# Eight order strings rewritten in a fused RWKV6 attention and GELU-MLP kernel

## The chip, the core and the metric

The kernel runs on one core of a Trainium2 chip. The time is the device time of one execution in microseconds (us). The median of three runs of the kernel before is given with its smallest and largest value. One further execution was recorded by the hardware profiler, and all views of the profile come from it.

A core has a matrix engine (TensorE, PE in the profile; its weight loads are shown as an engine of their own, PEld), a vector engine (VectorE, DVE), a scalar engine (ScalarE, ACT), GpSimd (POOL) and SyncE (SP), which in this kernel issues nearly all transfers. Each engine carries out its own list of instructions in order and waits at semaphores for the others. On TensorE the list is made of weight loads and matmuls; one fp32 matmul of the program shows as two weight loads and two matmuls in the trace, which is why the counts of the trace are twice those of the source.

## What is computed

There are four sequences of 768 tokens with eight heads of 48 channels. Each head runs a recurrence over time, and its output is the input of an MLP with the exact GELU:

```python
for t in range(S):                       # attention, per batch and head
    cur = einsum('bhd,bhe->bhde', u * kt, vt)
    y[:, :, t] = einsum('bhd,bhde->bhe', rt, state + cur)
    state = wt[..., None] * state + einsum('bhd,bhe->bhde', kt, vt)
x = y.transpose(0, 2, 1, 3).reshape(3072, 384)
h = x @ w_in                             # (384, 2048)
g = 0.5 * h * (1 + erf(h / sqrt(2)))
return g @ w_out                         # (2048, 384)
```

The weights come to the device in double precision and are turned to fp32 on the chip.

## The kernel before, in words

**Blocks.** The 3,072 tokens are cut into eight blocks of 384, and the program has one loop for each: in loop x the attention of block x runs beside the MLP of block x - 1. Within a block time is cut into chunks of 64 tokens, and the heads go in pairs, 12 chunk pairs for two pairs of heads.

**Attention of a block.** First the kernel lets VectorE multiply decay factors over growing stretches of time (`tot_sb`). In loops 0 and 1 the products of k and r within a chunk are then built level by level: TensorE multiplies blocks (`products`, L452, into a PSUM tile `d`), VectorE or ScalarE copies the valid part into `a_sb` (L513, L516), VectorE scales r and k with the decay (an `update`, L494 and L505), and the next level follows. Loops 2 to 7 use a shorter form with bursts of quarter blocks (L579, L588, copied at L604 and L621), ahead of which VectorE forms u r k (L391) and similar sums. Then come the transposes of k (L685, copied by ScalarE at L687 into `kx`), the products of k and v (L711, tile `kv_ps`), the chain of states on VectorE (L726, tile `st`), the part of y inside the chunks (L752, tile `y_ps`), two small copies that work as a fence on `y_ps` (L762, L764), the part of y from the states (L797), and the copies of y into `xT`, which the MLP reads. Some rows of y get to their place by small transfers on SP's and ScalarE's queues (L827). Loop 0 splits its attention into two units of two head pairs each, so that work can start when half of the data is there, and issues short matmuls on zeros (`keep_warm`, L225) between them.

**MLP of a block.** Block 0 goes through plain products: 16 steps of six matmuls in the trace into `h_ps` (L1059) with a GELU on ScalarE after each, then steps for the output (`o_ps`, L1153). Later blocks take a form with fewer multiplications, made of sums of weights (`w_sums` and `h_sums`, L844 to L888) and sums of x (`sums_of_x`, L897): products into `h_ps` and `u_ps` at L929, into `o_ps` at L1073.

**Weights.** w_in and w_out are 16 pieces of 768 KB. A piece is loaded by SP into a `raw` buffer (five of them; L200, the first three in shares of 256 KB at L205, each share behind a small memset on VectorE at L204). A conversion is three activations on ScalarE (L333, L334, L336) and two operations on VectorE (L345, L349), and its end issues the load of a later piece. So the order of the conversions also sets when SP issues loads. The rkw data of the next block are loaded in nine transfers of 384 or 256 KB (L176, `load`); those of block 1 in eight shares of 288 KB, each behind a memset on VectorE (L163 and L164, `load_second`).

**Where the order comes from.** All of this is written as generators that stop (`yield`) between steps; running a generator to its next stop issues the instructions of one step on all their engines. The string `PLAN[x]` decides, character by character, which generator takes its next step in loop x:

```python
for c in PLAN[x]:
    next(streams[c], None)
```

At the end of the string what is left in the loop's streams is run in a fixed order. The characters are:

- `.` a step of the MLP of block x - 1 (in loop 0: a step of unit 0 of the attention of block 0)
- `s` a step of the attention of block x (in loop 0: unit 1)
- `f` one of the first steps of the attention of block x + 1
- `l` a load for the next block (in loop 0: the gated shares of raw and of rkw)
- `c` a step of the conversions of weights (loops 0 and 1)
- `w` a step of the sums of weights (in loop 0: the load of v for block 1)
- `x` a step of the sums of x (in loop 0: matmuls on zeros)
- `p` in loop 0, the ScalarE part of a conversion alone

A step's instructions go to the ends of their engines' lists. The same steps in another order therefore do the same work, but each engine meets its waits in another order, and the transfers are issued at other places.

Of the kernel before, what the change touches and what calls it, by code (L numbers as in the profile page):

```python
# [36 lines left out]
NC_SP = 8  # L37
HALFWAY = 2
PLAN = {
    0: ".s...sl.ll.lclsllllssssl.lsl.l.ssl.lls..ssssc..s.sclcs.s..s..s.s.ss.s..csps.s.s.fpcfw",  # L40
    1: (
        "cs.c.cc.sslclcc.cs..ccswcc.sswccc.cccs.c.cccss.ccc.sc.scwlcclcsc.css.cs.clscsscclccc.sclls"
        "lc.wcc.ccfcccf.cc.s...fc.wcc.swcc.cc...cf.w.wwwx.xwxf.wl.f.xx"
    ),
    2: (
        "sw..sl..wss.....s..sws....ssw.wsw.sw.w.ss.lss..s.sw.ll.sw.s...ssls.s.s.ls..ss.s....s...sss"
        ".lsll.f.s.fs.ff..x.xl.xfxx"
    ),
    3: (
        "l.s.s..s...sls.ss....s...s.sss.ss.ss.ss...s.ssss..sssssssll....s....l..sl.sssls..llsf..sf."  # L50
        "ff.x.l.x.xfxx"
    ),
    4: (
        "sss...s..l....sl.s..s.s...l.ss..sss.l.s.s.ss.s.s...s.sl.ssl...sssss..s.....s.s..lss.sllfsf"
        "..lfs.f.f.x.x.xfxx"
    ),
    5: (
        ".ss...sss.l.....ss....sl.sssslss.s......sslss.sss..sssss..s..sl..s..s...s.lslsll.ssf.ff.s."
        ".x..x.lxxx"
    ),  # L60
    6: (
        "lls...ssss.s.s.s......l.s.s....s..sss.ssss.ss..sll..s...s..s..sss.s.sl.ss..s....slss.sl.lf"
        ".sf.f.s.ff..xx.xfxlx"
    ),
    7: "ss.ss.....s..s..s....s.ssss.ss...ss.s.ss..sss..sssss..s..s...s..s..s.s.sss..s.x..x..xxx",
}


# [1249 lines left out]
```

## Time and profile before

| | before |
|---|---|
| three runs | 590.59, 592.62 and 592.70 us; median 592.62 us |
| profiled execution | 592.35 us |
| its span, first to last instruction | 590.5 us |
| mean granted TensorE clock | 0.994 |
| TensorE busy, matmuls | 573.7 us (97%) |
| TensorE busy, weight loads | 521.3 us (88%), beside the matmuls |
| VectorE busy | 424.3 us (72%) |
| ScalarE busy | 290.8 us (49%) |
| GpSimd busy | 58.7 us (10%) |
| moved by DMA | 55.09 MB in 62,430 packets |

How to read it. "Busy" is the time within the span in which an engine carried out a counted instruction. The list of waits gives for an engine and a source line what the engine waited for ahead of that line: us in total, number of waits, the longest. "Issue" stands where the profile shows nothing that the engine waited for. Rows of the timeline give the start, the time, the engine, line, operation, output and input tiles and the number of instructions drawn together, with the idle time before them and its releaser in brackets. Rows of the windows give a stretch of time and its length; then busy time and number of instructions of TensorE's matmuls, its weight loads, VectorE, ScalarE and GpSimd; then the granted clock, the busy share of the DMA engines and the GB/s. Rows of the DMA queues give packets, MB and the share of the DMA engines' time in the window. Rows of the transfers give the issuing queue, the count, the KB of one and the median us from issue to landing. Rows of the groups give, behind the count, the busy time, the mean ns of one, and the idle time before them.

### The profile page before, as it was taken

The page shows a single profiled execution, that of the slowest core. Times are in us where ns is not written, and L with a number is a line of the kernel's source. Part 1 is how long each engine was busy: PE and PEld are TensorE (multiplying, and loading weights), DVE is VectorE, ACT ScalarE, POOL GpSimd, SP SyncE. Part 2 cuts the span into 40 slices and gives each one's busy share as a digit, 9 for nine tenths or more (in the row PEclk, how much of TensorE's full clock was granted, in tenths as well). Part 3 has the DMA queues.
Part 4 walks back from the last instruction along what each step waited for, and adds up shares of the span by engine and source line. Part 5 has one row for each costly group of instructions (what it writes and reads, how often), then busy time and mean ns, then how long its engine had stood idle before and what let it go on. Part 6 is the DMA issues. An engine that isn't in the chain of part 4 may idle for free. (4 is left out here: it accounts for less than half of the span.)

```text
span 590.5 us, 17675 instructions
## 1 busy us (share of the span) xinstructions
PE 573.7 (97%) x7616; PEld 521.3 (88%) x7616; DVE 424.3 (72%) x825; ACT 290.8 (49%) x668; POOL 58.7 (10%) x63
## 2 busy tenths in 40 slices
PE   6789999999999999999999999999999999999997
PEld 3476666699999989999999999999999999999997
DVE  6778768998959985687859986588859987420332
ACT  2258798535452467145652367246560466435400
POOL 3100000012000130011100130003100111003100
PEclk8999999999999999999999999999999999999999
DMA  7729645153232542445223432445213332114201
GB/s 253 255 80 319 214 159 163 44 125 80 26 68 68 122 56 37 132 145 100 29 54 116 107 53 42 111 138 92 28 34 108 81 48 40 30 44 54 28 13 35
DMA packets 62430, 55.09 MB, mean 93 GB/s; under 512 B 32400, under 2 KB 47504, under 8 KB 62352
## 3 DMA queue, kind: packets, MB, share of 16 engines
q1 hardware_dynamic: 50832, 45.62, 25.6%
q0 software_dynamic: 11424, 8.26, 10.7%
q8 instruction: 60, 0.98, 0.7%
q14 instruction: 18, 0.15, 0.1%
q10 hardware_dynamic: 96, 0.07, 0.1%
HBM read 36.24 MB, written 4.72 MB: 69 GB/s over the span
## 5 line engine op out<-in xcount | busy, mean ns | idle before, releaser
L929 PE MATMUL h_ps<-xT,w_in_sb 128*128 128x192 f32 x560 | 111.7, 331 | 0.7 <-DVE o_sb L1196 0.7
L980 POOL DMA_DIRECT2D g<-o_sb x42 | 50.7, 1250 | 482.0 <-ACT o_sb L965 473.4
L929 PEld LDWEIGHTS h_ps<-xT,w_in_sb 128*128 128x128 f32 x560 | 92.9, 190 | 5.0 <-ACT g L961 1.6
L929 PE MATMUL u_ps<-s,w_in_sb 128*128 128x192 f32 x224 | 41.2, 327 | 0.0
L1073 PE MATMUL o_ps<-w_out_sb,g 128*128 128x192 f32 x224 | 39.8, 326 | 0.0
L929 PEld LDWEIGHTS u_ps<-s,w_in_sb 128*128 128x128 f32 x224 | 37.1, 190 | 0.2
L1073 PEld LDWEIGHTS o_ps<-w_out_sb,g 128*128 128x128 f32 x224 | 37.0, 190 | 0.0
L604 ACT COPY a_sb<-d 32x256 f32<-32x256 f32 (+8 forms) x90 | 32.6, 363 | 4.2 <-PE d L588 2.7
L452 PEld LDWEIGHTS d<-rkw 64*64 64x64 f32 x1152 | 20.0, 142 | 16.1 <-issue 13.1
L1059 PE MATMUL h_ps<-xT,w_in_sb 128*128 128x384 f32 x96 | 32.6, 492 | 0.0
L1073 PE MATMUL o_ps<-w_out_sb,f 128*128 128x192 f32 x176 | 31.9, 330 | 0.0
L726 DVE SCALAR_TENSOR_TENSOR st<-st,tot_sb,kv_ps 128x48 f32<-128x48 f32 x160 | 29.0, 257 | 3.8 <-PE kv_ps L711 3.7
L1073 PE MATMUL o_ps<-t,g 128*128 128x192 f32 x176 | 31.3, 330 | 0.0
L1073 PE MATMUL o_ps<-t,s 128*128 128x192 f32 x176 | 31.3, 328 | 0.0
L1073 PE MATMUL o_ps<-w_out_sb,e 128*128 128x192 f32 x176 | 31.2, 328 | 0.0
L1073 PE MATMUL o_ps<-t,e 128*128 128x192 f32 x176 | 30.7, 327 | 0.0
L621 DVE COPY_PREDICATED a_sb<-quarter,d 128x480 f32<-128x480 uint8 (+5 forms) x54 | 23.1, 439 | 10.4 <-PE d L588 9.2
L1073 PEld LDWEIGHTS o_ps<-t,g 128*128 128x128 f32 x176 | 28.6, 190 | 0.5
L1073 PEld LDWEIGHTS o_ps<-w_out_sb,f 128*128 128x128 f32 x176 | 28.7, 190 | 0.4
L1073 PEld LDWEIGHTS o_ps<-t,s 128*128 128x128 f32 x176 | 28.8, 190 | 0.3
L1073 PEld LDWEIGHTS o_ps<-w_out_sb,e 128*128 128x128 f32 x176 | 28.8, 190 | 0.2
L1073 PEld LDWEIGHTS o_ps<-t,e 128*128 128x128 f32 x176 | 28.9, 190 | 0.1
(163 smaller groups left out, 1153.7 us busy)
## 6 DMA issues: line engine op xcount, KB each, us to landing
rkw<-in_rkw_dram SPq DMA_DIRECT2D x54, 256.0 KB, 3.6
g<-o_sb POOLq DMA_DIRECT2D x42, 192.0 KB, 3.6
raw<-in_w_out_dram SPq DMA_DIRECT2D x8, 768.0 KB, 4.7
v_in<-in_v_dram SPq DMA_DIRECT2D x8, 584.0 KB, 4.1
raw<-in_w_in_dram SPq DMA_DIRECT2D x5, 768.0 KB, 8.6
out_dram<-o_sb SPq DMA_DIRECT2D x20, 192.0 KB, 2.0
rkw<-kx SPq DMA_DIRECT2D x72, 48.0 KB, 2.0
rkw<-in_rkw_dram SPq DMA_DIRECT2D x6, 384.0 KB, 5.8
```

The source lines that it names most:

```text
L452: nc.tensor.matmul(d[half[p], g, n * width:(n + 1) * width], lhsT=kc[half[g], b, i, p], rhs=right(half[g], b, i, p), start=True, stop=True)
L604: nc.scalar.copy(out=at[z, g, first:behind, (a + 1) * h:], in_=d[z, :, :, to] if g == slice(None) else d[z, :, to])
L621: nc.vector.copy_predicated(out=an[:, :, :, :, (a + 1) * h:], mask=mask.to_broadcast(data.shape), data=data)
L726: nc.vector.scalar_tensor_tensor(out=stq[:, q, c], in0=stq[:, q, c - 1] if c else b4[:, q, NC - 1], scalar=totq[:, q, c:c + 1], in1=kvs[q ...
L929: nc.tensor.matmul(o, lhsT=lhsT, rhs=rhs, start=start, stop=True, skip_group_check=True)
L980: nc.gpsimd.dma_start(out=g, in_=z, accum_op=ALU.add)
L1059: nc.tensor.matmul(h_ps, lhsT=w_in_sb[:, f // FI, j, f % FI * 128:(f % FI + 1) * 128], rhs=xT[:, j, :], start=(j == 0), stop=(j == NJ - 1))
L1073: nc.tensor.matmul(o, lhsT=lhs(j), rhs=rhs(j), start=start and j == 0, stop=(j == HF - 1), skip_group_check=True)
```

## The change

Only the eight strings of `PLAN` are replaced. All steps stay what they are, and each stream holds the same steps in the same order among themselves; what differs is how the streams are interleaved. The whole diff:

```diff
--- before.py
+++ after.py
@@ -37,32 +37,32 @@
 NC_SP = 8
 HALFWAY = 2
 PLAN = {
-    0: ".s...sl.ll.lclsllllssssl.lsl.l.ssl.lls..ssssc..s.sclcs.s..s..s.s.ss.s..csps.s.s.fpcfw",
+    0: "l.s....llsl.lssslslss.lc.l.slslls...ssss..lcs.s.s.l.ss..ss..sccs.c.s.llpssslw..cs.ffpcc",
     1: (
-        "cs.c.cc.sslclcc.cs..ccswcc.sswccc.cccs.c.cccss.ccc.sc.scwlcclcsc.css.cs.clscsscclccc.sclls"
-        "lc.wcc.ccfcccf.cc.s...fc.wcc.swcc.cc...cf.w.wwwx.xwxf.wl.f.xx"
+        "..ccswccc.csl.scscs.s.sccwsc.clccs.ccsccc.csc.lscclswwclc.scs.wcssw.ss.cclcsc.ccs.lclccsc."
+        "ccclfccccccfccfcccccfccfccwf.ff......fw.sl.w.x.wx...x..x...xww"
     ),
     2: (
-        "sw..sl..wss.....s..sws....ssw.wsw.sw.w.ss.lss..s.sw.ll.sw.s...ssls.s.s.ls..ss.s....s...sss"
-        ".lsll.f.s.fs.ff..x.xl.xfxx"
+        "s.s.....ss....ssw.ws.wl.wsss.wws.s..lsl...lws.w..s.ww....s.s..l..sss.lssss....s..s..s.sls."
+        "llsf.sf.fs..fl.xx.x.fxx"
     ),
     3: (
-        "l.s.s..s...sls.ss....s...s.sss.ss.ss.ss...s.ssss..sssssssll....s....l..sl.sssls..llsf..sf."
-        "ff.x.l.x.xfxx"
+        "ls.ls....lss..ss.....ss..l.s.lsss.sss.s.s.s.ss..sss..sssssss....s.s..l...s..l.sslslsf.ffs."
+        "..x.lx..xxx"
     ),
     4: (
-        "sss...s..l....sl.s..s.s...l.ss..sss.l.s.s.ss.s.s...s.sl.ssl...sssss..s.....s.s..lss.sllfsf"
-        "..lfs.f.f.x.x.xfxx"
+        "lls.s.sss..s.l.........ssss.....sss.s.ss.s..s.sllss...s.s..l.sss.ss..s.ss...s..sslsll.s..f"
+        ".sf.sf..ff..xx.xflxx"
     ),
     5: (
-        ".ss...sss.l.....ss....sl.sssslss.s......sslss.sss..sssss..s..sl..s..s...s.lslsll.ssf.ff.s."
-        ".x..x.lxxx"
+        "..ss...s..ssl....sls...s.sss..sss..sss.sls...sllss..sssss.s..l..s.s...s.slll..s.ssfsf.fsf."
+        "....xxx.lxx"
     ),
     6: (
-        "lls...ssss.s.s.s......l.s.s....s..sss.ssss.ss..sll..s...s..s..sss.s.sl.ss..s....slss.sl.lf"
-        ".sf.f.s.ff..xx.xfxlx"
+        "ss..sss...s.....s.sl..s...l.s.ssls.s.s..s..sssssl......ss.ssss.sl.sl...s.....ss..llsssl.f."
+        "s.fsf.f.f.xx.l.xffxx"
     ),
-    7: "ss.ss.....s..s..s....s.ssss.ss...ss.s.ss..sss..sssss..s..s...s..s..s.s.sss..s.x..x..xxx",
+    7: "....ss.s...s.s.s....s.sss..ss.ss.sss..s..sss..sssssss......s.s....s..ssss.s...x.x..xxx",
 }
 
 
```

Read against the lists of the engines, it comes to this. In loop 0 TensorE's list is the same. The first share of raw (`l`) comes ahead of the first products, and the other shares are spread singly between steps of the attention; the VectorE halves of a conversion (L345, L349) come before the last two updates (L494), and the second pair of copies at L513 comes between the two copies at L687. In loop 1 the first five steps of the MLP of block 0 (L1059), which stood together behind the second products, are spread between the levels of the attention, with two ahead of the second products; conversions of weights shift by some steps, and three of the `f` steps stand behind the transposes of k. In loop 2 the first burst of quarters (L588) comes some steps earlier and the sums at L844 later. In loops 3 to 7 steps of `o_ps` (L1073) move across the products of k and v, the y products and the state products, four matmuls of the program at a time; in loop 5 the fence comes behind the four operations at L391 of the next block.

## The prediction

> **What bounds the kernel now.** I read the page's busy times first, then the waits of TensorE, then the order in time of loop 0, and last the DMA queues in short windows.
>
> ```profile
> PE 573.7 (97%) x7616; PEld 521.3 (88%) x7616; DVE 424.3 (72%) x825; ACT 290.8 (49%) x668; POOL 58.7 (10%) x63
> PE d L452 <- issue: 3.2, 2, 2.3
> PE kv_ps L711 <- issue: 1.5, 1, 1.5
> PE y_ps L752 <- DVE st L726: 1.3, 4, 0.4
> PE kv_ps L711 <- ACT kx L687: 0.6, 2, 0.3
> ```
>
> TensorE is busy 573.7 us of the span of 590.5. The changed program holds the same TensorE work, so only idle time can come or go: 16.8 us, of which the rows above carry the largest parts that order can touch. The two "issue" rows are unusual: TensorE has work, waits for no engine, and stands still. What they are shows in counts of instructions and in the queue that carries instructions:
>
> ```profile
> q8 instruction: 60, 0.98, 0.7%
> 0.00:18.80 18.80, 13.13 (x349) 7.88 (x350) 13.86 (x53) 6.67 (x9) 7.99 (x21) 0.91 0.79 254
> 0.00:25.00 25.00, 17.29 (x476) 10.43 (x477) 19.29 (x63) 6.67 (x9) 7.99 (x21) 0.93 0.85 283
> 0.00:43.10 43.10, 32.33 (x986) 21.99 (x989) 31.51 (x101) 15.82 (x27) 7.99 (x21) 0.92 0.60 199
> 0.00:46.60 46.60, 35.83 (x1113) 24.47 (x1114) 34.61 (x107) 18.04 (x32) 7.99 (x21) 0.93 0.60 195
> ```
>
> In each row the two counts behind the first times are TensorE's matmuls and weight loads. The first two windows end inside the two L452 gaps: 699 and 953 have begun, a step of 254. Queue q8 brings 60 packets for 15,232 of them, 254 each. So TensorE stops at a packet's edge when the next packet has not come. By steps of 254 to 255 further edges fall at about 1717, 1972 (loop 1 starts at 43.1, with 1975) and 2227 (46.6). When the packet comes late:
>
> ```profile
> q1 hardware_dynamic: 763, 1.46, 103.8%
> q8 instruction: 1, 0.02, 29.4%
> 25.85 0.62 PE L452 MATMUL d<-rkw 64*64 64x64 f32 x26 [2.27 <-issue]
> q1 hardware_dynamic: 763, 1.57, 85.0%
> q8 instruction: 1, 0.02, 18.5%
> ```
>
> The first q1 row is the window 19.4 to 23.4: no q8 packet, 1.46 MB of loads. Its q8 row is the window 23.4 to 23.6. TensorE had crossed the edge before at 19.4 and ran on at 25.85. The second pair is 46.75 to 52.3 and 52.3 to 52.6: the edge at 2227 is crossed at 46.75, and again 1.57 MB of loads go first. I read from both: a packet is asked for when the edge before it is crossed, goes behind the loads that are already issued, and can be used 2.4 us after it starts (23.45 to 25.85).
>
> **The change part by part.** No operation is added or removed; orders alone differ.
>
> Loop 0, loads. Before 21.6 us the old order issues eight shares of raw (256 KB) and eight of rkw (288 KB). The new one puts the first raw share ahead of the block products and spreads the others singly; by the same step on VectorE six and six are out. That is two of each less, 1.11 MB (from the KB below). Of the 1.46 MB ahead of the packet 0.35 are left, so the wait of 4.1 us falls to about 1.0 and the packet is usable at 19.4 + 1.0 + 2.4 = 22.8, before its need at 23.6 (25.85 less 2.27). The gap of 2.27 us goes. The gap at 18.8 is hidden today behind VectorE; I book nothing for it.
>
> ```profile
> rkw<-in_rkw_dram SPq DMA_DIRECT2D x8, 288.0 KB, 5.6
> raw<-in_w_in_dram SPq DMA_DIRECT2D x9, 256.0 KB, 5.6
> 22.47 0.60 PE L225 MATMUL warm<-zeros 128*128 128x512 bf16 x2
> 26.40 0.89 PE L225 MATMUL warm<-zeros 128*128 128x512 bf16 x2
> 23.88 0.55 DVE L516 COPY_PREDICATED a_sb<-mask,d 128x384 f32<-128x384 uint8 x1
> 26.50 0.96 DVE L505 TENSOR_TENSOR rkw<-rkw,tot_sb 128x768 f32<-128x768 f32 x1 [2.08 <-PE d L452]
> 31.20 0.93 PE L452 MATMUL d<-rkw 64*64 64x64 f32 x48
> 33.59 0.95 ACT L513 COPY a_sb<-d 32x384 f32<-32x384 f32 x2 [0.45 <-PE d L452]
> 33.90 1.47 PE L685 MATMUL kt_ps<-ident,rkw 128*128 128x128 f32 x12
> 34.76 1.50 ACT L687 COPY kx<-kt_ps 128x768 f32<-128x768 f32 x2 [0.21 <-PE kt_ps L685]
> 35.61 0.92 PE L711 MATMUL kv_ps<-v_in,kx 64*64 64x48 f32 x48 [0.23 <-ACT kx L687]
> ```
>
> What is late next is VectorE. After L516 ends at 24.43 come L505 (0.96), L516 (0.55) and two L505 (1.92): 27.9. The last block products follow, 28.5 to 29.4 (0.93 after a warm pair of 0.60), the update of k (half an L505, 0.5), kt at 30.0, its copy by ScalarE 0.86 later (34.76 less 33.90), 0.75 long. The new order has two L513 copies (0.95) between the two L687 copies, and kv waits for them: 30.9 + 0.75 + 0.95 + 0.2 = 32.8 in place of 35.61, a lead of 2.8. L345 and L349 move ahead of the last two updates; VectorE then ends near 33, before kv is done, so they cost nothing. The gap of 1.5 at the next edge has no load beside it (kv crosses its edge and the packet comes in its own time): it stays. Bounds of the lead: 0 if the packet is still late, 3.7 if nothing but TensorE counts (2.27, and 1.4 of matmuls that ran slowly after the gap, as 0.89 against 0.60 shows).
>
> Loop 1, start. Two mlp steps (four of the five were grouped) now come before the second 96 products.
>
> ```profile
> 46.07 0.44 PEld L452 LDWEIGHTS d<-kx,rkw 64*64 64x64 f32 x24 [0.42 <-ACT kx L401]
> 55.96 1.60 PE L452 MATMUL d<-rkw 64*64 64x32 f32 x96
> 44.68 1.47 PE L225 MATMUL warm<-zeros 128*128 128x512 bf16 x6
> 48.02 8.01 PE L1059 MATMUL h_ps<-xT,w_in_sb 128*128 128x384 f32 x24
> xT<-ysb ACTq DMA_DIRECT2D x3, 24.0 KB, 4.2
> 42.02 1.87 SPq L827 DMA_DIRECT2D xT<-ysb  x3
> 43.99 0.59 SPq L156 DMA_DIRECT2D v_in<-in_v_dram  x1
> ...
> 47.22 3.50 SPq L200 DMA_DIRECT2D raw<-in_w_in_dram  x3
> ```
>
> Loop 1's products start at 43.1 today; call it S. The first mlp step would start at S + 3.0 and wants xT, whose last transfers are issued at S + 0.5 and land 4.2 later: about 0.5 us of a new wait. The small wait at S + 3.0 (0.4 for the weight load, some 0.3 of TensorE), where the second products stand behind kx today, go.
>
> The edges move too. From S: 192 instructions of products, 12 warm, 24 of two mlp steps, so the edge at 254 is 26 instructions into the second products, at S + 1.6 + 1.4 + 4.0 + 0.5 + 0.2 = S + 7.7. To the next one lie the other 166, 24 of two mlp steps, and 64 of the next products: 1.4 + 4.0 + 0.5 later, S + 13.6. Today the same two edges are at S + 3.7 and S + 13.2. SP's row of loads is longer by one raw share and starts at the same place, right after xT: 256 + 584 + 3 x 768 + 2 x 256 KB, 3.74 MB. All are issued before S + 7.7, since no wait but the landing of xT stands among them. Today 0.5 MB moved from S + 0.8 to S + 3.7 and then:
>
> ```profile
> 46.75:56.30 9.55, 9.53 (x121) 6.00 (x120) 9.21 (x12) 8.04 (x15) 0.00 (x0) 1.00 0.93 332
> v_in<-in_v_dram SPq DMA_DIRECT2D x8, 584.0 KB, 4.1
> raw<-in_w_in_dram SPq DMA_DIRECT2D x5, 768.0 KB, 8.6
> rkw<-in_rkw_dram SPq DMA_DIRECT2D x54, 256.0 KB, 3.6
> L391 DVE SCALAR_TENSOR_TENSOR kx<-rkw,u_sb,rkw 128x384 f32<-128x384 f32 x12 | 9.3, 891 | 0.5 <-issue 0.2 <-DMA rkw<-in_rkw_dram 0.2
> ```
>
> At 332 GB/s the 3.74 MB are through at S + 3.7 + 9.8 = S + 13.5; the packet starts there and is usable at S + 15.9, 2.3 us after TensorE needs it. Ends: 0, if the packet goes earlier, and 7 (a rival below). I take 2.2. The following packet has about half the loads ahead of it and some 6 us to come: 0.3.
>
> Rest of loop 1: conversions move by a step or two, three mlp steps come between kt and L711, which hides the second L687 wait (0.3). The products of w_out come after more conversions; ScalarE, which sets their pace, does the same work in the same stretch, so 0.
>
> Loops 2 to 7. Of the four y_ps waits (1.3) three get four to eight more o_ps matmuls in front, which covers them: -1.0. In loop 5 the fence now follows the four L391 instead of preceding them (0.89 each), with some matmuls of o_ps as cover; no row shows how many of the 3.6 us stay open, and I take +0.3. Loads, sums and L588 move by a step; nothing of TensorE waits long there today; unchanged.
>
> Sum: -2.8 + 0.5 - 0.3 + 2.2 + 0.3 - 0.3 - 1.0 + 0.3 = -1.1. The profiled execution took 592.35, 0.27 under the median of 592.62, so 591.25 in its terms, and **591.4** for a median.
>
> **The rivals.** First, the packet in loop 1 does not stay behind the whole row of loads: 2.2 and 0.3 fall away, 588.9. For it: packets at other places start within a microsecond. Against it: at 46.75 and 19.4 none went before the loads. DMA: Bandwidth & Descriptors in the Trainium skill (Queues, rings and completion order) states that an engine turns from queue to queue after each packet, which speaks for this rival; by it the sum would be 588.9, and 1.57 MB ahead of one packet disagree.
>
> Second, slower: the same packet is dearer. If the seventh raw load (768 KB), which waits only for a conversion that ends near S + 7.2, also goes ahead, 4.5 MB are out. In 46.75 to 52.3 the rate was only 1.57 MB in 5.55 us, 0.283 per us; at the edge some 1.6 MB have moved, and 2.9 at that rate take 10.4. The packet is usable at S + 20.5, 6.9 late: 591.25 - 2.5 + 6.9 = 595.7. It decides from about 2.7 MB ahead.
>
> Third, loop 0's packet is still late and VectorE gains nothing: 591.4 + 2.8 = 594.2.
>
> Fourth, the packets have nothing to do with the gaps. Then neither 2.8 nor 2.5 count: 591.7. Runtime: NRT & Kernel Launch in the Trainium skill (Instruction fetch mechanics) gives TensorE room for 2048 instructions ahead and calls fetches mostly hidden; the edges at every 254 with gaps of up to 2.27 disagree.
>
> **How the numbers follow.** 0.5% is 3.0 us, about what a measurement of this kernel can tell from no change: bounds 589.7 and 595.6. Forecast 0.44, first rival 0.29, second 0.13, third 0.10, fourth 0.04. Faster 0.29 plus a little of the forecast's tail, 0.30; slower 0.13; same 0.57. The forecast's own range is 589.7 to 593.5; with the rivals 588.0 to 595.8, the low end by a lead of 3.7 in loop 0 without the packet's wait.
>
> **What would show it.** In loop 0 the "issue" gap of 2.3 us is gone and kv_ps starts near 32.8, the first L452 of loop 1 near 40.3. About 13.6 after that, L452 shows a new "issue" gap near 2 us, with a q8 packet behind full DMA slices. L1059 shows a short wait for xT. y_ps L752 waits for st in one loop only. A gap of 2 us at loop 0's second edge, or none in loop 1, would refute a step.

## The result and the profile after

The changed kernel takes 590.17 us (median of 22 runs, 586.87 to 593.38); the kernel before 592.59 (22 runs, 590.44 to 595.28). The ratio is 0.9954, 95% interval 0.9937 to 0.9971: 2.7 us faster by the ratio, 2.4 by the two medians. Forecast were 591.4 and a gain of 1.1 us against the profiled run. At one mean granted clock, 0.997, the kernel before took 593.0 us on average (23 executions, recorded beside the experiments) and the changed one 590.4 (16), so the clock does not make the gain. The profiled execution took 589.61 us with a span of 587.8, against 592.35 and 590.5 before.

TensorE's busy row and its list of waits in the changed kernel:

```profile
PE 571.1 (97%) x7602; PEld 521.4 (89%) x7616; DVE 425.5 (72%) x825; ACT 291.2 (50%) x668; POOL 58.6 (10%) x63
PE d L452 <- DMA rkw<-in_rkw_dram: 3.5, 1, 3.5
PE d L452 <- issue: 1.8, 2, 1.4
PE kv_ps L711 <- issue: 1.0, 1, 1.0
PE o_ps L1073 <- issue: 0.5, 1, 0.5
PE y_ps L752 <- DVE st L726: 0.3, 1, 0.3
PE kv_ps L711 <- ACT kx L687: 0.2, 1, 0.2
```

"Issue" at L452 fell from 3.2 to 1.8 us, the y_ps waits from 1.3 to 0.3, kv's wait for kx from 0.6 to 0.2. One wait is new: 0.5 us of "issue" at o_ps. The 14 matmuls that the busy row lacks (7602 against 7616 weight loads) are records missing from the trace, so I compare stretches by their length and not by busy time. The windows of both traces, cut where the same work was done (start, start of loop 1's products, the 49th weight load of L1153, end):

```profile
43.10:109.90 66.80, 66.35 (x1132) 43.46 (x1129) 53.45 (x89) 57.44 (x93) 0.00 (x0) 1.00 0.57 191
109.90:590.50 480.60, 475.01 (x5508) 455.82 (x5506) 339.33 (x637) 217.56 (x549) 50.74 (x42) 1.00 0.32 70
```

```profile
0.00:41.55 41.55, 29.79 (x976) 21.96 (x989) 31.86 (x102) 15.75 (x27) 7.99 (x21) 0.96 0.63 201
41.55:107.50 65.95, 65.90 (x1123) 43.26 (x1124) 56.56 (x93) 57.61 (x94) 0.00 (x0) 1.00 0.56 197
107.50:587.80 480.30, 475.37 (x5507) 456.14 (x5506) 337.09 (x632) 217.88 (x548) 50.64 (x42) 1.00 0.32 70
```

The first pair of rows is before (its loop 0, 43.10, stands in the prediction), the other after. Loop 0 gained 1.55 us where 2.8 were forecast; loop 1 gained 0.85 where the forecast had a loss of 2.4; the rest gained 0.3 where it had 0.7. So the total came close to the forecast by two errors of opposite sign. The timeline of TensorE, two rows of before and then those of after, shows both. (The first edge of loop 0 is the packet's edge at 699 instructions, the second the one at 953, and kv's edge lies in the kv products.)

```profile
8.75 0.96 PE L452 MATMUL d<-rkw 64*64 64x64 f32 x48 [2.87 <-DMA rkw<-in_rkw_dram]
19.41 0.33 PE L452 MATMUL d<-rkw 64*64 64x64 f32 x3 [0.97 <-issue]
```

```profile
9.43 1.56 PE L452 MATMUL d<-rkw 64*64 64x64 f32 x48 [3.55 <-DMA rkw<-in_rkw_dram]
21.09 0.33 PE L452 MATMUL d<-rkw 64*64 64x64 f32 x3 [1.42 <-issue]
25.60 0.62 PE L452 MATMUL d<-rkw 64*64 64x64 f32 x26 [0.35 <-issue]
33.89 0.91 PE L711 MATMUL kv_ps<-v_in,kx 64*64 64x48 f32 x48 [0.23 <-ACT kx L687]
37.43 0.20 PE L711 MATMUL kv_ps<-v_in,kx 64*64 64x48 f32 x1 [0.96 <-issue]
41.56 1.60 PE L452 MATMUL d<-rkw 64*64 64x32 f32 x96
44.40 4.03 PE L1059 MATMUL h_ps<-xT,w_in_sb 128*128 128x384 f32 x12
48.36 1.63 PE L452 MATMUL d<-kx,rkw 64*64 64x64 f32 x96
```

The gap of 2.27 us at loop 0's second edge is down to 0.35. But the first products start 0.7 us later than before (9.43 against 8.75) and take 1.56 us in place of 0.96, and the gap at the first edge grew from 0.97 to 1.42. In loop 1 no gap is left: L1059, the second products and what follows run on without a wait.

A part of loop 0's difference is neither gap nor order. From the second edge to kt's transposes the same 228 weight loads took 8.05 us before and 6.58 after, with no wait for another engine in between. The rows of these windows, before and after, differ in the granted clock, 0.79 against 1.00:

```profile
25.85:33.90 8.05, 8.05 (x229) 5.08 (x228) 4.71 (x8) 3.73 (x11) 0.00 (x0) 0.79 0.34 105
25.60:32.18 6.58, 5.95 (x223) 4.35 (x228) 4.74 (x10) 3.42 (x10) 0.00 (x0) 1.00 0.45 123
```

Before, the clock reads 0.50 from 26.6 to 30.0 us, and after, 0.50 from 9.4 to 11.0 us, where the slow first products lie. So these two traces compare loop 0 at different clocks.

### The profile page after: what moved, and what is told of

It reads as the page before. It is cut to its first block, busy times and chain, and to the rows that moved or that the text cites. A ratio compares the mean times of both kernels' runs of the same rounds, so it can differ in the third digit from the quotient of the medians.

```text
span 587.8 us, 17656 instructions
## 1 busy us (share of the span) xinstructions
PE 571.1 (97%) x7602; PEld 521.4 (89%) x7616; DVE 425.5 (72%) x825; ACT 291.2 (50%) x668; POOL 58.6 (10%) x63
## 5 line engine op out<-in xcount | busy, mean ns | idle before, releaser
L1073 PE MATMUL o_ps<-w_out_sb,g 128*128 128x192 f32 x224 | 39.8, 326 | 0.0
L1073 PEld LDWEIGHTS o_ps<-w_out_sb,g 128*128 128x128 f32 x224 | 37.0, 190 | 0.0
L1059 PE MATMUL h_ps<-xT,w_in_sb 128*128 128x384 f32 x96 | 33.2, 494 | 0.0
L452 PEld LDWEIGHTS d<-rkw 64*64 64x64 f32 x1152 | 19.4, 138 | 14.7 <-issue 10.5
L1073 PE MATMUL o_ps<-w_out_sb,f 128*128 128x192 f32 x176 | 32.0, 331 | 0.0
L1073 PE MATMUL o_ps<-t,g 128*128 128x192 f32 x176 | 31.4, 330 | 0.0
L1073 PE MATMUL o_ps<-t,s 128*128 128x192 f32 x176 | 31.2, 328 | 0.0
L1073 PE MATMUL o_ps<-t,e 128*128 128x192 f32 x176 | 30.6, 326 | 0.5 <-issue 0.5
L1073 PE MATMUL o_ps<-w_out_sb,e 128*128 128x192 f32 x176 | 30.7, 328 | 0.0
L982 DVE TENSOR_TENSOR g<-g,o_sb 128x384 f32<-128x384 f32 x14 | 7.6, 549 | 31.2 <-ACT o_sb L965 31.1
L1073 PEld LDWEIGHTS o_ps<-t,e 128*128 128x128 f32 x176 | 28.9, 190 | 0.7 <-issue 0.7
L1073 PEld LDWEIGHTS o_ps<-t,g 128*128 128x128 f32 x176 | 28.6, 190 | 0.5
L1073 PEld LDWEIGHTS o_ps<-w_out_sb,f 128*128 128x128 f32 x176 | 28.5, 190 | 0.6
L1073 PEld LDWEIGHTS o_ps<-t,s 128*128 128x128 f32 x176 | 28.8, 190 | 0.2
```

Of the source, the lines that this page charges most:

```text
L452: nc.tensor.matmul(d[half[p], g, n * width:(n + 1) * width], lhsT=kc[half[g], b, i, p], rhs=right(half[g], b, i, p), start=True, stop=True)
L982: nc.vector.tensor_add(g, g, z)
L1059: nc.tensor.matmul(h_ps, lhsT=w_in_sb[:, f // FI, j, f % FI * 128:(f % FI + 1) * 128], rhs=xT[:, j, :], start=(j == 0), stop=(j == NJ - 1))
L1073: nc.tensor.matmul(o, lhsT=lhs(j), rhs=rhs(j), start=start and j == 0, stop=(j == HF - 1), skip_group_check=True)
```

## The experiments

My theory after the result: the loads that are out when TensorE asks for an instruction packet set how late it is; the first share of raw, issued ahead of the first products, cost loop 0 the missing 1.2 us; and loop 1's packet did not stall because not all loads go ahead of it.

### One part of the change at a time

Loop 0 alone, on the kernel before:

```diff
-    0: ".s...sl.ll.lclsllllssssl.lsl.l.ssl.lls..ssssc..s.sclcs.s..s..s.s.ss.s..csps.s.s.fpcfw",
+    0: "l.s....llsl.lssslslss.lc.l.slslls...ssss..lcs.s.s.l.ss..ss..sccs.c.s.llpssslw..cs.ffpcc",
     1: (
-        "cs.c.cc.sslclcc.cs..ccswcc.sswccc.cccs.c.cccss.ccc.sc.scwlcclcsc.css.cs.clscsscclccc.sclls"
+        "s..cc.sslclcc.cs..ccswcc.sswccc.cccs.c.cccss.ccc.sc.scwlcclcsc.css.cs.clscsscclccc.scllslc"
...
```

> The kernel before with the new order of loop 0 alone (loop 1's string without the two conversion steps that loop 0 now takes). By the two traces loop 0 ends 1.6 us earlier (41.5 in place of 43.1) and nothing behind it changes: 1.6 us faster. The prediction's step for loop 0 said 2.8. If the first share of raw, issued ahead of the first products, is what delays the first L452, that L452 starts near 9.4 here as in the changed kernel; if its 0.7 us were chance, it starts near 8.75 and loop 0 ends near 40.6.

Measured: ratio 0.9964 (0.9944 to 0.9984), 2.1 us faster. The first L452 started at 9.17, between the two values, and loop 0 ended at 40.5, where I had put it if the late start were chance. Loops 1 and 2 alone:

```diff
     1: (
-        "cs.c.cc.sslclcc.cs..ccswcc.sswccc.cccs.c.cccss.ccc.sc.scwlcclcsc.css.cs.clscsscclccc.sclls"
-        "lc.wcc.ccfcccf.cc.s...fc.wcc.swcc.cc...cf.w.wwwx.xwxf.wl.f.xx"
+        "cc..ccswccc.csl.scscs.s.sccwsc.clccs.ccsccc.csc.lscclswwclc.scs.wcssw.ss.cclcsc.ccs.lclccs"
+        "c.ccclfccccccfccfcccccfccfccwf.ff......fw.sl.w.x.wx...x..x...xww"
     ),
     2: (
...
+        "s.s.....ss....ssw.ws.wl.wsss.wws.s..lsl...lws.w..s.ww....s.s..l..sss.lssss....s..s..s.sls."
+        "llsf.sf.fs..fl.xx.x.fxx"
```

> The kernel before with the new orders of loops 1 and 2 alone. By the two traces loop 1 gains 0.8 us and loop 2 nothing: 0.8 us faster, no issue gap of TensorE in loop 1. By the prediction's step a packet in loop 1 comes 2.2 us late: then 1.3 us slower, with an issue gap near 13 us after loop 1's start.

Measured: 0.9987 (0.9969 to 1.0004), no difference that can be told. In loop 1 (window 41 to 112 of its trace) TensorE's only wait is this:

```profile
PE d L452 <- issue: 0.3, 1, 0.3
```

The prediction's 2.2 us of stall in loop 1 is refuted a second time; 0.3 of "issue" came. Loops 3 to 7 alone:

```diff
     3: (
-        "l.s.s..s...sls.ss....s...s.sss.ss.ss.ss...s.ssss..sssssssll....s....l..sl.sssls..llsf..sf."
-        "ff.x.l.x.xfxx"
+        "ls.ls....lss..ss.....ss..l.s.lsss.sss.s.s.s.ss..sss..sssssss....s.s..l...s..l.sslslsf.ffs."
+        "..x.lx..xxx"
     ),
...
-    7: "ss.ss.....s..s..s....s.ssss.ss...ss.s.ss..sss..sssss..s..s...s..s..s.s.sss..s.x..x..xxx",
+    7: "....ss.s...s.s.s....s.sss..ss.ss.sss..s..sss..sssssss......s.s....s..ssss.s...x.x..xxx",
```

> The kernel before with the new orders of loops 3 to 7 alone. By the two traces these gain 0.3 us: three waits of y_ps for st go (0.9), and an issue gap of 0.5 to 0.7 at o_ps near 450 us comes. The prediction said 0.7 of gain. Either way within 1 us of before. If the issue gap near 450 is not there, it was not this order that made it.

Measured: 0.9973 (0.9959 to 0.9986), 1.6 us faster, more than either number expected; the interval, 0.8 to 2.4 us, holds the 1.0 that the y_ps waits are worth. Its waits have

```profile
PE y_ps L752 <- DVE st L726: 0.3, 1, 0.3
```

and no "issue" at o_ps. So the y_ps waits went as forecast (1.0 us), and these loops alone don't bring the new wait at o_ps.

The traces of these two kernels hold the old loop 0 twice more, the first holds the new one again. The gaps at the second edge and the first products of loop 1, in turn for loop 0 alone (the second edge has no "issue" row there; the first edge's row is shown), loops 1 and 2 alone, loops 3 to 7 alone:

```profile
20.20 0.33 PE L452 MATMUL d<-rkw 64*64 64x64 f32 x3 [0.21 <-issue]
40.55 1.71 PE L452 MATMUL d<-rkw 64*64 64x32 f32 x96
```

```profile
24.63 0.62 PE L452 MATMUL d<-rkw 64*64 64x64 f32 x26 [1.45 <-issue]
40.73 0.25 PE L452 MATMUL d<-rkw 64*64 64x32 f32 x2
```

```profile
26.38 0.62 PE L452 MATMUL d<-rkw 64*64 64x64 f32 x26 [1.72 <-issue]
43.36 0.25 PE L452 MATMUL d<-rkw 64*64 64x32 f32 x2
```

The old order's second gap is 2.27, 1.45 and 1.72. The new order's is 0.35 in the changed kernel, and in the five other traces that hold the new loop 0 (loop 0 alone here, and four below) no "issue" row stands there. That step is shown. All "issue" gaps at the edges of loop 0 together, kv's included, are 4.7, 4.7 and 4.9 us in the three traces of the old order and 1.6 to 3.1 in the six of the new.

But the same old loop 0 ends at 43.1, 40.7 and 43.4: it varies by 2.6 us between executions, as much as the change is worth. The sums of gaps just given are not what varies. From the second edge to kt, loops 1 and 2 alone, then loops 3 to 7 alone, read:

```profile
24.63:31.21 6.58, 5.94 (x223) 4.35 (x228) 4.65 (x8) 3.72 (x11) 0.00 (x0) 1.00 0.33 96
26.38:34.45 8.07, 7.01 (x224) 4.97 (x229) 4.70 (x8) 3.72 (x11) 0.00 (x0) 0.79 0.29 94
```

The two longer loops each have two stretches of 3.4 us in which the granted clock reads 0.50 (9.5 to 12.9 and 26.6 to 30.0 us before, 9.9 to 13.3 and 27.0 to 30.4 in loops 3 to 7 alone); the short one has none. The second stretch is worth 1.5 us by these rows. The first is worth 0.6: from the first products to the fifth set of them it took 5.9 us before, 5.3 in loops 1 and 2 alone and 5.9 in loops 3 to 7 alone. The rest, 0.3 and 0.4, is a later start. So one pair of traces can't size loop 0; the timed ratio can, at 2.1 us with an interval of some 1.2 to either side, and the gaps in sum agree with it (4.8 less 2.6 on average).

### The first share of raw

```diff
-    0: "l.s....llsl.lssslslss.lc.l.slslls...ssss..lcs.s.s.l.ss..ss..sccs.c.s.llpssslw..cs.ffpcc",
+    0: ".s....lllsl.lssslslss.lc.l.slslls...ssss..lcs.s.s.l.ss..ss..sccs.c.s.llpssslw..cs.ffpcc",
```

> The changed kernel with one character moved: the first share of raw goes with the second and third, behind the first products, in place of ahead of them. If that share delayed the start (first L452 at 9.43 against 8.75, then slow matmuls after the longer idle time), loop 0 is 1.2 us shorter than the changed kernel's, and the kernel 1.2 us faster than the changed one, 3.9 faster than before. Rival: the later start is chance, and the first L452 starts at 9.4 again or at 8.75 in both; then it is as fast as the changed kernel.

Measured: 0.9947 (0.9927 to 0.9967) against 0.9954 for the changed kernel: the same. Its loop 0:

```profile
8.02 1.56 PE L452 MATMUL d<-rkw 64*64 64x64 f32 x48 [2.12 <-DMA rkw<-in_rkw_dram]
20.14 0.33 PE L452 MATMUL d<-rkw 64*64 64x64 f32 x3 [1.88 <-issue]
42.62 0.25 PE L452 MATMUL d<-rkw 64*64 64x32 f32 x2
```

The first products started early, at 8.02, and the time was lost again: at the first edge (1.88 against 1.42 in the changed kernel), in a stretch of granted clock 0.50 behind it (1.5 us longer from there to the second edge), and at kv's edge (1.89 against 0.96). (The first products took 1.56 here too, though the clock reads 1.00 in 8.0 to 9.6 us; that early, the time of the matmuls is the surer sign.) My theory of the share falls as far as the end is concerned. Whether the share delays the start stays open: with it ahead the first L452 began at 9.0 to 10.3 in seven traces, without it at 8.0 to 9.9 in six, and these overlap.

### Do loads make the packets late?

Of the kernel before, only the loads of loop 0 go where the change has them:

```diff
-    0: ".s...sl.ll.lclsllllssssl.lsl.l.ssl.lls..ssssc..s.sclcs.s..s..s.s.ss.s..csps.s.s.fpcfw",
+    0: "l.s...sll.l.lcssslsls.sl.l.slsll.s..ssssc..ls.sccs.sl..s..s.s.ss.s..llcsps.ls.s.fpcfw",
```

> The kernel before with the loads of loop 0 alone moved to the places that they have in the changed kernel; conversions and the load of v stay. If the loads are what delays the packets, the second L452 gap (2.27, 1.45 and 1.72 in three traces of the old order) is under 0.5 and loop 0 ends within 0.7 us of the run with the whole new order of loop 0 (40.4); the kernel is some 2 us faster than before. If the other moves of loop 0 make the gain, the gap may go but loop 0 ends near 42.5.

```profile
24.34 0.62 PE L452 MATMUL d<-rkw 64*64 64x64 f32 x26 [0.62 <-issue]
37.50 0.20 PE L711 MATMUL kv_ps<-v_in,kx 64*64 64x48 f32 x1 [2.17 <-issue]
41.35 1.60 PE L452 MATMUL d<-rkw 64*64 64x32 f32 x96
```

Measured: 0.9990 (0.9976 to 1.0004). The second gap fell to 0.62, as by the theory, if not under 0.5, and loop 0 ended at 41.35, between the two values expected; but kv's gap grew to 2.17, all "issue" gaps of loop 0 together are 4.0, and the gain of 2 us did not come. Loads that are taken from one edge stand before another: in the window 33.3 to 35.1 the queues moved 0.37 MB of loads ahead of the packet for kv's edge, which started 1.9 us after the edge before it; in the kernel before, with no load there, it started 0.9 us after. The opposite test takes them all away: fourteen of the seventeen loads, and the conversions, go behind the last products.

```diff
-    0: ".s...sl.ll.lclsllllssssl.lsl.l.ssl.lls..ssssc..s.sclcs.s..s..s.s.ss.s..csps.s.s.fpcfw",
+    0: ".s...llls..sssss.s..ss.s..ssss..s.ss.s..s..s.s.ss.s..llllllllllllllss.s.s.ccccccppffw",
```

> The kernel before with fourteen of the seventeen loads of loop 0 moved behind the last products, and the conversions behind them. Nothing is left out, but loop 1 will wait for its data, so the total is no measure. If the loads are what makes the packets late, both issue gaps of L452 in loop 0 (0.97 to 1.97 and 1.45 to 2.27 us in three traces of the old order) are under 0.3 and kt's transposes start near 30 in place of 33.9. If packets are late whatever the loads, the gaps stay over 0.9.

```profile
9.91 1.56 PE L452 MATMUL d<-rkw 64*64 64x64 f32 x48 [4.02 <-DMA rkw<-in_rkw_dram]
31.03 1.47 PE L685 MATMUL kt_ps<-ident,rkw 128*128 128x128 f32 x12
37.65 0.20 PE L711 MATMUL kv_ps<-v_in,kx 64*64 64x48 f32 x1 [2.54 <-issue]
```

Both L452 gaps are gone: no "issue" row stands between these first two rows. From the first products to kt it takes 21.1 us (31.03 less 9.91) against 25.2 before (33.90 less 8.75) and 22.8 and 25.6 in the other two traces of the old order; 1.5 us of the two longer times are the stretch of half clock. The moved loads now make the next gaps, 2.54 at kv and 1.8 at the edge behind it. The conversions moved too in this run, but not in the one before, where the second gap fell with the loads alone. It is the loads. (The whole took 602.3, since loop 1 waited 5.4 us for the late data.)

Could loop 0 be tuned by this? First the changed kernel with the old loops 1 and 2, then its loads in groups behind the times of asking:

```diff
     1: (
-        "..ccswccc.csl.scscs.s.sccwsc.clccs.ccsccc.csc.lscclswwclc.scs.wcssw.ss.cclcsc.ccs.lclccsc."
+        "s..cc.sslclcc.cs..ccswcc.sswccc.cccs.c.cccss.ccc.sc.scwlcclcsc.css.cs.clscsscclccc.scllslc"
...
     2: (
-        "s.s.....ss....ssw.ws.wl.wsss.wws.s..lsl...lws.w..s.ww....s.s..l..sss.lssss....s..s..s.sls."
+        "sw..sl..wss.....s..sws....ssw.wsw.sw.w.ss.lss..s.sw.ll.sw.s...ssls.s.s.ls..ss.s....s...sss"
...
```

> The changed kernel with the old orders of loops 1 and 2 put back: new orders in loop 0 and loops 3 to 7. Loop 0 alone gave 2.85 us and loops 3 to 7 alone 1.6. If the parts add up, 4.4 us faster than before, 588.2. Rival: the changed kernel is only 2.7 faster because the parts do not add, for another reason than loops 1 and 2; then again about 590. The issue gap at o_ps near 445 us of the changed kernel should be absent if the new loops 1 and 2 moved the packets' edges there.

Measured: 0.9955 (0.9935 to 0.9976), as the changed kernel's 0.9954. So no cost and no gain of the new loops 1 and 2 can be told. The two parts alone would multiply to 0.9937 (0.9964 times 0.9973), which lies inside the interval: whether they add up in full is not settled. The "issue" gap at o_ps is absent, as expected, but loops 1 and 2 alone do not show it either, so what makes it stays open. With the loads in groups:

```diff
-    0: "l.s....llsl.lssslslss.lc.l.slslls...ssss..lcs.s.s.l.ss..ss..sccs.c.s.llpssslw..cs.ffpcc",
+    0: ".s....llls.sssslllss.c..sllllss...sssllls..csll.s.s..ss..ss..llsccs.c.s.psssw..cs.ffpcc",
```

> The kernel of the run before this one with loop 0's loads in other places: three shares of raw behind the first products, then three, four, three, two and two shares, each group set on VectorE behind the time at which TensorE asks for a packet. If late packets come from loads that are out when they are asked for, the two L452 issue gaps of loop 0 (0.2 to 2.3 us in the traces so far) are both under 0.5 and loop 0 ends 0.5 to 1 us earlier than in the run before; if packets do not care for loads, the gaps stay as they are.

```profile
29.96 0.93 PE L452 MATMUL d<-rkw 64*64 64x64 f32 x48 [1.64 <-DVE rkw L505]
39.93 0.20 PE L711 MATMUL kv_ps<-v_in,kx 64*64 64x48 f32 x1 [2.99 <-issue]
```

A miss: 0.9977 (0.9960 to 0.9993), 1.3 us slower than the run before it by the two ratios, whose intervals overlap a little. The "issue" gaps at the first two edges are gone, but the third edge shows 1.64 (the row names L505, which had ended 0.9 us before the matmuls started) and kv's 2.99, and loop 0 ended at 43.7. Ahead of the packet at kv's edge, in the window 34.6 to 37.5, the loads were these:

```profile
q1 hardware_dynamic: 485, 0.93, 93.0%
```

SP issues the groups later than VectorE allows them (two shares of raw that it allows at 21.7 go out from 23.8 on), so they drift into the next packet's time.

### Why loop 1's packet was not late

The packet of the edge inside loop 1's second products (TensorE crosses it near 48.5) was to start behind 3.74 MB. In the changed kernel q1 reads, for 48.5 to 50.3, and q8, for 50.3 to 50.5:

```profile
q1 hardware_dynamic: 323, 0.63, 99.9%
q8 instruction: 1, 0.02, 27.5%
```

The packet started at 50.4, not at 55, with 0.63 MB moved since the crossing while the engines stayed full: it passed loads. Two causes could do that: it is asked for earlier than I thought, or it doesn't wait for all that is out. Two kernels take the loads away.

```diff
             if not gate:
+                if 4 <= i <= 7:
+                    w8 = dst.shape[2] // 8
+                    nc.gpsimd.memset(dst.bitcast(U32)[:, :, 2 * w8:], 0)
+                    dst, src = dst[:, :, 0:w8], src[:, :, 0:w8]
                 nc.sync.dma_start(out=dst, in_=src)
```

> The changed kernel with four loads of raw in loop 1 (the third to sixth piece loaded whole, 768 KB each) cut to an eighth and the rest of the buffer set to zero by GpSimd, so the weights of those pieces are left out. In the changed kernel the packet asked for at the edge that TensorE crosses at 48.5 started at 50.4. If it is asked for at the crossing, it starts here 0.6 to 1 us after the crossing (near 49.3), never before. If it is asked for some 3 us before the crossing, when the sequencer runs ahead of the slow L1059 matmuls, and only waited behind the loads, it starts before the crossing, near 46 to 47.

```diff
-        dma.dma_start(out=loaded[x][1], in_=v[x])
+        n = v.shape[2] // (8 if x == 1 else 1)
+        if x == 1:
+            nc.gpsimd.memset(loaded[x][1][:, n:], 0.0)
+        dma.dma_start(out=loaded[x][1][:, 0:n], in_=v[x][:, 0:n])
```

> The kernel of the run with small loads in loop 1 (four pieces of raw cut to an eighth, the rest zeros), with the load of v for block 1 cut to an eighth too (the rest of v zeros, so block 1's attention leaves most of v out). There the packet started 0.3 us after the crossing at 47.4, with 1.2 MB of loads before it since xT came. If it is asked for when the sequencer has run through the twelve L1059 matmuls (near 44.4, right after xT's wait ends) and goes behind the loads out then, it starts here near 45, over 2 us before its edge is crossed. If it is asked for at the crossing and passes loads in turns, it starts again 0.3 us or more after the crossing.

With small loads of raw the packet started in the window 47.65 to 47.8, some 0.3 us after its crossing, which is 26 instructions into these products (L456 is L452 there). That is neither of the two outcomes expected, and settles nothing:

```profile
q8 instruction: 1, 0.02, 36.6%
47.28 1.63 PE L456 MATMUL d<-kx,rkw 64*64 64x64 f32 x96
```

With v small too it started in the window 49.4 to 49.6, ahead of the second products themselves (49.62), and so ahead of the edge inside them; q1 of 48.0 to 49.4, q8 of 49.4 to 49.6, then the row of TensorE (L459 is L452 there):

```profile
q1 hardware_dynamic: 513, 0.36, 87.3%
q8 instruction: 1, 0.02, 27.4%
49.62 1.63 PE L459 MATMUL d<-kx,rkw 64*64 64x64 f32 x96
```

So the asking runs ahead of the crossing: shown, by one execution. It does so by less than the "over 2 us" that I expected, as the start itself was only 0.3 us early; how much of that time the packet stood behind the small loads is not known. And a packet doesn't wait for everything that is out. The kernel with the late loads shows that at the same edge, where TensorE had stood 5.4 us for kx right before and could not run ahead; q1 of 54.9 to 58.7, q8 of 58.7 to 58.95:

```profile
q1 hardware_dynamic: 800, 1.54, 105.2%
q8 instruction: 1, 0.02, 25.4%
```

SP had issued 3.3 MB more than had been moved at the crossing (summed from its issues and q1's bytes); 1.5 went first. Summed in the same way over the first 110 us of all thirteen traces: where up to 1.35 MB was out, most or all of it went first, save where the packet started at the crossing and had been asked for before those loads; where more was out, 1.0 to 1.6 MB went first. At this one edge in the changed loop 1 only 0.2 to 0.7 MB of 2.2 to 2.45 was moved since the crossing; a request one to two microseconds ahead, at 0.35 MB per us, would bring that nearer to the others, but that is worked out, not shown.

The Trainium skill, DMA: Bandwidth & Descriptors (Queues, rings and completion order), says that an engine drains a whole packet of one queue, up to 64 descriptors, before it turns to the next. The 800 pieces ahead of the packet above are 50 for each of 16 engines, which agrees with a bound of that size; no run here shows how the pieces are grouped. The prediction set its 1.57 MB against this rule, but 763 pieces are 48 for each engine, which such a bound allows.

### The changed kernel once more

> The changed kernel once more, for the spread between executions of one program. Loop 0 ended at 41.6 in its first trace; three traces of the old order gave 43.1, 40.7 and 43.4. I expect it within 1.5 us of 41.6, no issue gap in loop 1, and one y_ps wait for st.

```profile
41.79 0.25 PE L452 MATMUL d<-rkw 64*64 64x32 f32 x2
PE kv_ps L711 <- DMA rkw<-kx: 0.8, 1, 0.8
```

591.0 us, span 589.2. Loop 0 ended at 41.8, loop 1 had no "issue" gap, y_ps one wait of 0.3, as expected. In loop 1 L1059 waited 0.6 us, near the 0.5 that the prediction had for xT; the row names L411, so the cause is not shown. The 0.5 us of "issue" at o_ps is not there; near the same place, in loop 6, kv waited 0.8 us for a transfer instead. So some 0.5 to 0.8 us go there in both traces of the changed kernel, by different waits; why is open.

## Why the prediction was right, and where it was wrong

**Direction and time.** 590.17 lies in the range, 1.2 us under the forecast of 591.4, between it and the first rival's 588.9. (The prediction's own sum, 1.1 off 592.62, is 591.5.) That it came so near is luck in part: loop 1 was wrong by 3.25 us one way, loop 0 and the rest by 1.65 the other.

**The mechanism of packets and loads** holds: taking the loads away takes both L452 gaps away. The third and the fourth rival fall. The packet that TensorE asks for at the first edge went behind 1.46 MB before; after, behind 0.24 in the window 21.2 to 22.2, and it starts in 22.2 to 22.4:

```profile
q1 hardware_dynamic: 132, 0.24, 65.5%
q8 instruction: 1, 0.02, 56.2%
```

**Loop 0, "a lead of 2.8"**: right in the packet, wrong in what follows it. The gap fell from 2.27 to 0.35, but kv started at 33.89 and not at 32.8. Three things were booked at nothing that are not nothing: the start, later by 0.7; the first products at half clock, some 0.55 up to the first edge; and the gap there, which grew by 0.45. None is stable from one execution to the next. With the 0.35 they put kt at 32.18 and not at 30.0. "What is late next is VectorE" did not come true: TensorE's rows show no wait from 25.60 to kt. Nor did "kv waits for them": kv's first products stand behind the first L687 copy alone.

```profile
33.04 0.80 ACT L687 COPY kx<-kt_ps 128x768 f32<-128x768 f32 x1 [1.61 <-PE kt_ps L685]
```

It ends at 33.84, and kv starts at 33.89, while ScalarE is still at the two L513 copies (33.73 to 34.67). So from kt to kv it took 1.71 us, as before, and not 2.8. The slow matmuls behind the gap, 1.4 us that the prediction's kt at 30.0 takes as gained, are the stretch of half clock. They went in this pair of traces, but the kernel with loops 1 and 2 alone has the old gap (1.45) without them, so they do not always come with it. The timed gain of the part alone is 2.1 us.

**Loop 1, "I take 2.2"**: this is the step that failed, at "at 332 GB/s the 3.74 MB are through at S + 13.5; the packet starts there". It started at 50.4, which is S + 8.8. A packet can be asked for ahead of its crossing where slow matmuls stand before the edge, and 1.0 to 1.6 MB at most went before it, however much was out. The first rival had the outcome right, though it gave no bound. With it the following packet's 0.3 falls too. The second rival, a dearer packet, fell with the missing gap in loop 1; by the bound, 1.6 MB at the slowest rate seen, 0.283 per us, are 5.6 us, and its 10.4 came in no trace.

**Waits.** No wait of TensorE's matmuls for xT came in the profiled execution (0.5 forecast). The small wait at the second products and most of kv's wait for kx went, as forecast. The y_ps waits went from 1.3 to 0.3, as forecast to a tenth. The fence in loop 5 cost nothing (0.3 forecast). What was not forecast is the 0.5 to 0.8 us in loop 6.

**The whole**, by the profiled executions: loop 0 gained 1.25 less than forecast and loops 2 to 7 0.4 less; loop 1 came out 3.25 better. That is 1.6 us better than the forecast of 1.1, the 2.7 that was measured.

## What to carry to other kernels

Where TensorE stands still for "issue", count its instructions to the place: if the gaps lie a fixed number apart, look in the instruction queue for the packet and in the load queue for what goes before it. Spread large loads so that little is out when short matmuls run through a packet's worth of instructions in a few microseconds, as in loop 0 here; in front of loop 1's slow matmuls loads of 2.4 MB cost nothing. Moving loads moves the gap to the next such edge, so add up all the gaps and test by timed ratio, not by the one gap that you aimed at. And look at the granted clock stretch by stretch before you set two traces side by side: 0.994 against 1.000 over this whole kernel was 0.92 against 1.00 over loop 0, and 2.1 us.

## What the runs showed that was not expected

- A late packet has a bound in these traces: 1.0 to 1.6 MB went first at most, 1.5 with 3.3 MB out.
- The same instructions of loop 0 took 40.7, 43.1 and 43.4 us in three executions. The gaps at the edges do not make the difference; two stretches of 3.4 us at a granted clock of 0.50 make 2.1 us of it, in the two longer loops alone. What brings such a stretch on in one execution and not in another, no run settles.
- The gap at kv's edge (1.2 to 1.8 us in the three traces of the old order, 0.8 to 2.1 in the six of the new) needs no load: before, no load was out there, and still TensorE stood 1.5 us, since the 254 instructions up to that edge run in about 2 us, less than a packet takes to come.
